# Zero halves of five query and key buffers: written by transfers in ScalarE's queue instead of by the engines

## The chip, the cores and the metric

The kernel runs on one core of a Trainium2 chip. The metric is the device time of one execution in microseconds (us). Executions are timed from outside, and one further execution is recorded by the hardware profiler, which gives the trace that is read here.

## The reference

Two layers in float32, one after the other:

```python
# attention: q, k, v of (B 4, H 8, S 768, D 64); 8 global keys, a window of 96
scores = (q @ k.T) / sqrt(D) - slope[h] * dist      # dist is capped at n_local for global keys
scores = where(is_global | is_local, scores, -1e9)
a = exp(scores - max); a = a / (sum(a) + 1e-9)
x = (a @ v)  # heads side by side: (B, S, 512)
# channel mix: x_prev is x moved by one position
xk = mu_k * x + (1 - mu_k) * x_prev;  xr = mu_r * x + (1 - mu_r) * x_prev
out = sigmoid(xr @ w_r) * (relu(xk @ w_k) ** 2 @ w_v)
```

The weights are float64 values, which the kernel gets as pairs of 32-bit words and turns into float32 itself.

## The kernel before

The sequence is cut into 24 tiles of 128 queries (B times NT = 6). One loop of steps goes over the tiles. In a step the tile's scores are made for two heads at a time (`scores`, matmuls of L421 and L422 into the PSUM tile `s`), VectorE adds the bias pattern and takes the maximum (L430), ScalarE takes the exponential (L431), TensorE turns the result (`transposes`, L461), ScalarE copies it out (L465), and `weighted` multiplies it by v (L486). The channel mix of a pair of tiles (`ffn`, lines L529 to L531) is fed in between. Ten blocks of weight words are loaded in the first steps (L181, L182; 1 MB each), put together on VectorE (L210 to L212), and split into a high and a low part (L216 on ScalarE, L230 to L234 on TensorE, ScalarE and VectorE).

The first six tiles are "native": their scores are float32 matmuls over 128 partitions, of which the 64 even ones hold q or k (`qr[0:128:2]`, loaded by L338 and L339 from SyncE's queue) and the 64 odd ones must be zero. Their buffers are used in turn: two query buffers `q_zero[0]`, `q_zero[1]` (in the trace `qz`) and three key buffers `k_ring[0]` to `k_ring[2]` (`kz`). They are zeroed once, ahead of the first loads, by `zero_fill`: the table `PLAN["Z"]` names an engine for each, D for VectorE (L311), A for ScalarE (L309, two instructions a buffer), and GpSimd where the table says nothing (L306). A whole buffer is zeroed, so that the load of its even partitions must come behind.

At the start VectorE also makes the distances for the bias patterns: GpSimd writes counters (`iota`, L136 to L138), L139 turns them into floats in `btmp`, L78 takes in the two sizes (`sizes_w`, loaded by the first transfer in SyncE's queue, L71), and the chain ends in L149 and L164. From these, ScalarE, VectorE and GpSimd make `pat0` (L153, L155) and `pat` (L170, L172); ScalarE also makes `minus` (L85), which only the weights need. `mus` (L89) is the first transfer in ScalarE's queue. Ten matmuls on `zeros` (L116) run on TensorE while it has nothing else to do.

The order within each engine is not the order of the code: a scheduler sets it by a model of the times, but for SyncE's queue, which is kept in program order for the first six steps. Each engine then works through its list in order. Transfers share eight completion semaphores, DMAHW0 to DMAHW7, which are given out in turn; a transfer waits before it is issued for the last user of its semaphore to land.

Of the kernel before, what the change touches and what calls it, by code (L numbers as in the profile page):

```python
# [9 lines left out]
F32 = mybir.dt.float32  # L10
# [9 lines left out]
B, H, S, D = 4, 8, 768, 64  # L20
# [8 lines left out]
W = GMAX + BACK + 128  # L29
# [7 lines left out]
PLAN = {  # L37
    "HI": 'AAAAAAAAAA',
    "LOW": 'PPDPDDDDDD',
    "RC": 'AAAAAAAAAAAAAAAAAAAA',  # L40
    "ER": set(),
    "ET": (),
    "XC": (),
    "Z": {('q', 0): 'D', ('q', 1): 'A', ('k', 1): 'A'},
    "P0": 'DADDADAD',
    "GD": 0,
    "GO": (1, 1),
# [15 lines left out]
def tile_biased_attention_channel_mix(ctx: ExitStack, tc: tile.TileContext, qT, kT, v, n_sizes, mu_kr, w_k, w_v, w_r, q_rows, k_rows, v_rows, slopes, out):  # L63
    nc = tc.nc
    vec, act, pool, pe = nc.vector, nc.scalar, nc.gpsimd, nc.tensor
# [16 lines left out]
    ident = const.tile([128, 128], F32, name="ident")  # L82
    make_identity(nc, ident)
    minus = const.tile([128, 128], F32R, name="minus")
    nc.scalar.mul(minus, ident, -1.0)  # L85

    mus = const.tile([128, 2, 4], F32, name="mus")
    mus1 = const.tile([128, 2, 4], F32, name="mus1")
# [8 lines left out]
    kw_pool = fast.enter_context(tc.tile_pool(name="kw", bufs=2))  # L97
    q_pool = fast.enter_context(tc.tile_pool(name="qp", bufs=2))
# [13 lines left out]
    zeros = const.tile([128, 256], BF16, name="zeros")  # L112
# [3 lines left out]
        pe.matmul(idle, zeros[:, 0:128], zeros.unsqueeze(1).broadcast_to([128, 2, 256]), start=True, stop=True)  # L116

    pat = const.tile([128, H, W], BF16, name="pat")
# [177 lines left out]

    state = {}  # L300


    def zero_fill(which, i, whole):
        e = PLAN["Z"].get((which, i), "P")
        if e == "P":
            pool.memset(whole, 0.0)  # L306
        elif e == "A":
            for h in (0, 4):
                act.copy(whole[:, h : h + 4, :], zeros[:, 0:128].unsqueeze(1).broadcast_to([128, 4, 128]))  # L309
        else:  # L310
            vec.memset(whole, 0.0)  # L311

    q_zero, k_ring = [], []
    for i in range(3):
        if i < 2:
            q_zero.append(q_pool.tile([128, H, 128], F32, name=f"qz_{i}", tag="qh"))
            kz = kw_pool.tile([128, H, W], F32, name=f"kz_{i}", tag="kw").rearrange("p h w -> p (h w)")[:, 0 : H * 128]
            kz = kz.rearrange("p (h w) -> p h w", h=H)
            zero_fill("q", i, q_zero[i])
        else:  # L320
            kz = q_pool.tile([128, H, 128], F32, name=f"kz_{i}", tag="ql")
        zero_fill("k", i, kz)
        k_ring.append(kz)
    k_first = const.tile([128, H, GMAX], F32, name="k_first")

    def first_keys(n):
# [516 lines left out]
```

## Time and profile before

| | us |
|---|---|
| median of 3 runs | 499.98 (498.32 to 500.26) |
| the profiled execution | 496.85 |
| its span, from the first to the last instruction | 495.1 |
| TensorE busy in the span | 485.0 (98%) |
| VectorE busy | 348.9 (70%) |
| ScalarE busy | 335.8 (68%) |

1.75 us of the profiled execution lie outside the span. TensorE is busy nearly throughout, but busy shares are means over stages with different limits, so the first stage has to be read by itself.

### The profile page before, as it was taken

Reading aid. Unit: us, or ns where it says so; the run is one execution under the profiler, and the core shown is the slowest. Engines: PE = TensorE matmul, PEld = TensorE weight load, DVE = VectorE, ACT = ScalarE, POOL = GpSimd, SP = SyncE. Lnnn points to the kernel's source line nnn. Section 1 sums busy time; section 2 is a strip of 40 time slices with the busy share of each in tenths; the row PEclk is TensorE's granted clock in tenths of the full one; section 3 lists DMA queues with packets and bytes.
Section 4 is the critical chain, followed back from the end, with each engine's and each line's share of the span. In section 5 each row is a group of like instructions: output and inputs, shape, how many; then the busy total and the mean of one; then the engine's idle time right before and its main releaser. Section 6 shows DMA issues by size and latency. Waiting matters only on the chain.

```text
span 495.1 us, 10282 instructions
## 1 busy us (share of the span) xinstructions
PE 485.0 (98%) x3614; PEld 432.1 (87%) x3614; DVE 348.9 (70%) x839; ACT 335.8 (68%) x852; POOL 204.2 (41%) x331
## 2 busy tenths in 40 slices
PE   7999999999999999999999999999999999999995
PEld 5688988998988988988988998998998998988984
DVE  7999988857577777667677677777677656446431
ACT  8999866557397478468488578477487477595450
POOL 4202043638375454554564554644655633203000
PEclk9999999999999999999999999999999999999998
DMA  6997343811525216216306306406405125574401
GB/s 249 377 312 305 71 93 82 208 45 38 135 73 136 65 47 169 77 36 153 103 24 158 94 4 167 122 2 161 129 2 139 49 72 165 185 263 164 144 25 51
DMA packets 22587, 60.59 MB, mean 122 GB/s; under 512 B 3296, under 2 KB 4576, under 8 KB 22016
## 3 DMA queue, kind: packets, MB, share of 16 engines
q1 hardware_dynamic: 22384, 59.85, 41.1%
q8 instruction: 31, 0.51, 0.4%
q14 instruction: 28, 0.23, 0.1%
q10 hardware_dynamic: 144, 0.00, 0.0%
HBM read 53.55 MB, written 6.29 MB: 121 GB/s over the span
## 4 chain that ended last, share of the span: by engine, by line
PE 95%; DVE 2%; ACT 1%; issue 0%; ACTq 0%
PE kp L529 9%; PE kp L530 9%; PE kp L531 9%; PE vps L529 9%; PE vps L531 9%; PE vps L530 9%; PE av L486 8%; PE t L461 8%; PE z L529 5%; PE z L530 4%; PE z L531 4%; PE s L425 3%; PE s L424 3%; PE s L422 2%; PE s L421 2%; PE rest L230 1%
## 5 line engine op out<-in xcount | busy, mean ns | idle before, releaser
L449 POOL TENSOR_SCALAR e<-e,r 128x232 f32<-128x232 f32 (+1 forms) x144 | 68.7, 495 | 122.8 <-DVE r L443 86.8
L431 ACT ACTIVATE e<-e,nmax 128x232 f32<-128x232 f32 (+1 forms) x192 | 89.6, 469 | 36.7 <-DVE nmax L430 36.1
L529 PE MATMUL kp<-xk_hi,wk 128*128 128x256 f32 x384 | 107.9, 282 | 0.0
L530 PE MATMUL kp<-xk_lo,wk 128*128 128x256 f32 x384 | 107.3, 280 | 0.0
L531 PE MATMUL kp<-xk_hi,wk 128*128 128x256 f32 x384 | 107.2, 280 | 0.0
L430 DVE CUSTOM_DVE_ANT_0 e<-s,pat 128x232 f32<-128x232 f32 (+1 forms) x192 | 64.2, 374 | 27.9 <-PE s L425 25.8
L529 PE MATMUL vps<-wv,kk_hi 128*128 128x512 f32 (+1 forms) x200 | 76.8, 385 | 0.0
L531 PE MATMUL vps<-wv,kk_lo 128*128 128x512 f32 (+1 forms) x200 | 76.7, 383 | 0.0
L530 PE MATMUL vps<-wv,kk_hi 128*128 128x512 f32 (+1 forms) x200 | 76.4, 382 | 0.0
L530 PEld LDWEIGHTS kp<-xk_lo,wk 128*128 128x128 f32 x384 | 72.1, 188 | 0.8 <-DVE xk_lo L522 0.2
L529 PEld LDWEIGHTS kp<-xk_hi,wk 128*128 128x128 f32 x384 | 72.0, 188 | 0.7 <-ACT xk_hi L521 0.3
L531 PEld LDWEIGHTS kp<-xk_hi,wk 128*128 128x128 f32 x384 | 72.1, 188 | 0.0
L465 ACT COPY et<-t 128x256 f32<-128x256 f32 (+1 forms) x176 | 53.3, 354 | 23.4 <-PE t L461 23.2
L461 PE MATMUL t<-ident,e 128*128 128x128 f32 x352 | 54.5, 275 | 0.4 <-ACT et L465 0.3
L557 DVE TENSOR_TENSOR kk<-kp,kk 128x512 f32<-128x512 f32 x48 | 32.9, 688 | 29.8 <-ACT kk L556 29.4
L559 DVE TENSOR_TENSOR kk_lo<-kk,kk_hi 128x512 fp32r<-128x512 f32 x48 | 36.7, 769 | 24.1 <-ACT kk_hi L558 23.2
L461 PEld LDWEIGHTS t<-ident,e 128*128 128x128 f32 x352 | 40.3, 135 | 6.2 <-ACT et L465 0.6
L558 ACT CAST kk_hi<-kk 128x512 fp32r<-128x512 f32 x48 | 29.7, 622 | 22.2 <-DVE kk L557 21.9
L531 PEld LDWEIGHTS vps<-wv,kk_lo 128*128 128x128 f32 x200 | 37.6, 188 | 7.5
L529 PEld LDWEIGHTS vps<-wv,kk_hi 128*128 128x128 f32 x200 | 37.6, 189 | 6.7 <-issue 0.2
L530 PEld LDWEIGHTS vps<-wv,kk_hi 128*128 128x128 f32 x200 | 37.7, 189 | 6.5
L424 PE MATMUL s<-kw,qh 128*128 128x232 f32 (+1 forms) x144 | 40.4, 306 | 0.0
(119 smaller groups left out, 1068.2 us busy)
## 6 DMA issues: line engine op xcount, KB each, us to landing
qraw<-in_qT_dram SPq DMA_DIRECT2D x36, 256.0 KB
kraw<-in_kT_dram SPq DMA_DIRECT2D x36, 256.0 KB
out_dram<-sig SPq DMA_DIRECT2D x23, 256.0 KB
va<-in_v_dram SPq DMA_DIRECT2D x20, 240.0 KB
vb<-in_v_dram SPq DMA_DIRECT2D x20, 208.0 KB
w<-in_w_k_dram SPq DMA_DIRECT2D x4, 1024.0 KB
w<-in_w_v_dram SPq DMA_DIRECT2D x4, 1024.0 KB
again<-in_w_k_dram SPq DMA_DIRECT2D x8, 512.0 KB
```

Source lines behind the costliest of these rows:

```text
L424: pe.matmul(o, s["qh"][:, h, :], s["kw"][:, h, c0:W], start=True, stop=False)
L430: biased[n, hp] = vec.tensor_tensor_reduce(out=e[:, :w], in0=o, in1=p[:, h, :], op0=ALU.add, op1=ALU.min, scale=-0.125, scalar=3.0e38, acc ...
L431: act.activation(e[:, :w], e[:, :w], AF.Exp, bias=s["nmax"][:, h : h + 1], scale=-1.0, accum_out=s["sum"][:, h : h + 1])
L449: pool.tensor_scalar(e[:, :w], e[:, :w], r[:, u : u + 1], 1.0, op0=ALU.mult, op1=ALU.mult)
L461: s["turned"] = pe.transpose(pt[0:p, c : c + 128], e[:, k * 128 : k * 128 + p], ident)
L465: act.copy(dst, pt[0:p, k * 256 : k * 256 + 256].rearrange("p (u q) -> p u q", u=2)[:, :, q:128])
L486: pe.matmul(o, vt[:, h * 64 : (h + 1) * 64], et[0:p, c : c + 128 - q], start=k == 0, stop=k == nb - 1)
L529: pe.matmul(o, sh, mh, start=first, stop=False)
L530: pe.matmul(o, sh, ml, start=False, stop=False)
L531: pe.matmul(o, sl, mh, start=False, stop=last)
L557: vec.tensor_mul(kk, pv, kk)
L559: rest = vec.tensor_sub(kkl[:, 2 * fp : 2 * fp + 2, :], kk, kkh[:, 2 * fp : 2 * fp + 2, :])
```

## The change

The zeros of all five buffers come from transfers. Each is issued from ScalarE's queue and copies 512 bytes of zeros, eight times for each partition, from 64 partitions of the tile `zeros` into the 64 odd partitions of a buffer: 64 x 8 pieces of 512 bytes, 256 KB a buffer. The even partitions are no longer written beforehand. The code of `zero_fill` stands further ahead, and `minus` is put behind the last of the five transfers.

```diff
-    "Z": {('q', 0): 'D', ('q', 1): 'A', ('k', 1): 'A'},
+    "Z": {('q', 0): 'S', ('k', 0): 'S', ('q', 1): 'S', ('k', 1): 'S', ('k', 2): 'S'},
...
     minus = const.tile([128, 128], F32R, name="minus")
-    nc.scalar.mul(minus, ident, -1.0)
...
+    filled = []
+
+    def zero_fill(which, i, whole):
+        e = PLAN["Z"].get((which, i), "P")
+        if e == "P":
+            pool.memset(whole, 0.0)
+        elif e == "S":
+            filled.append(nc.scalar.dma_start(whole[1:128:2], zeros.bitcast(F32)[0:64].unsqueeze(1).broadcast_to([64, H, 128])))
...
+    with tc.issue_after(filled[-1].ins):
+        act.mul(minus, ident, -1.0)
```

The first rows of ScalarE's list before (each row a line of the code, an operation, and what it writes and reads; semaphores that it waits for in brackets):

```order
L89 DMA mus<-in_mu_kr_dram 128x8
L309 ACT_TABLE_LOAD
L309 CAST qz_182<-zeros 128x512 [waits DVE_49]
L309 CAST kz_183<-zeros 128x512 x2
L85 ACTIVATE minus<-ident 128x128 [waits Pool_49]
L153 ACTIVATE pat_137<-btmp 128x128 [waits DVE_49]
L170 ACTIVATE pat<-btmp 128x232 [waits DVE_49]
```

And with the change, where line numbers differ (L127 is the new transfer, L181 the old L153, L198 the old L170; qz_135 and qz_139 are the two query buffers, kz_136, kz_140 and kz_143 the three key buffers):

```order
L88 DMA mus<-in_mu_kr_dram 128x8
L127 DMA qz_135<-zeros 64x8x128 [waits DVE_49]
L127 DMA kz_136<-zeros 64x8x128
L127 DMA qz_139<-zeros 64x8x128
L127 DMA kz_140<-zeros 64x8x128 [waits DMAHW1_49]
L127 DMA kz_143<-zeros 64x8x128 [waits DMAHW3_49]
L146 ACT_TABLE_LOAD
L146 ACTIVATE minus<-ident 128x128 [waits Pool_49]
L181 ACTIVATE pat_147<-btmp 128x128 [waits DVE_49]
L198 ACTIVATE pat<-btmp 128x232 [waits DVE_49]
```

Ahead of the table load stand five transfers in place of one, and two of them wait for the landing of an earlier transfer; the table load and the patterns moved behind these waits.

SyncE's list before, from its second transfer on:

```order
L338 DMA qz_178<-in_qT_dram 64x1024 [waits DVE_49]
L339 DMA kz_179<-in_kT_dram 64x1024 [waits Pool_49]
L338 DMA qz_182<-in_qT_dram 64x1024 [waits Activation_49]
L339 DMA kz_183<-in_kT_dram 64x1024 [waits Activation_49]
L374 DMA va_199<-in_v_dram 128x512
L181 DMA w_0_211<-in_w_k_dram 128x2048
L181 DMA w_1_213<-in_w_k_dram 128x2048 [waits DMAHW0_49]
L338 DMA qz_178<-in_qT_dram 64x1024 [waits DMAHW2_49,DMAHW1_49,PE_49]
L339 DMA kz_188<-in_kT_dram 64x1024 [waits Pool_49]
```

And with the change (L344 is the old L338, L345 the old L339, L209 the old L181):

```order
L344 DMA qz_135<-in_qT_dram 64x1024
L345 DMA kz_136<-in_kT_dram 64x1024
L344 DMA qz_139<-in_qT_dram 64x1024
L345 DMA kz_140<-in_kT_dram 64x1024 [waits DMAHW0_49]
L380 DMA va_197<-in_v_dram 128x512 [waits DMAHW2_49]
L209 DMA w_0_209<-in_w_k_dram 128x2048 [waits DMAHW4_49]
L209 DMA w_1_211<-in_w_k_dram 128x2048 [waits DMAHW5_49]
L344 DMA qz_135<-in_qT_dram 64x1024 [waits DMAHW6_49,PE_49]
L345 DMA kz_143<-in_kT_dram 64x1024 [waits DMAHW7_49]
```

The order is the same. The waits for the zeroing engines are gone, and the transfers from the fourth on now wait for the landing of earlier transfers.

TensorE's list at the first scores, before:

```order
L422 MATMUL s_0_202<-kz_179,qz_178 128x128 [waits DMAHW2_49,DMAHW3_49,DVE_49,Pool_49]
L422 MATMUL s_3_255<-kz_179,qz_178 128x128 [waits DVE_49]
L461 MATMUL t_0_274<-ident,e_0_205 128x128 [waits Activation_49]
L461 MATMUL t_1_306<-ident,e_2_224 128x128 [waits Activation_49]
L421 MATMUL s_0_279<-kz_179,qz_182 128x104 [waits DMAHW4_49,DVE_49,Pool_49]
L422 MATMUL s_0_279<-kz_183,qz_182 128x128 [waits DMAHW5_49]
```

And with the change (L428 is the old L422, L427 the old L421, L467 the old L461):

```order
L428 MATMUL s_0_200<-kz_136,qz_135 128x128 [waits DMAHW4_49,DMAHW5_49,DMAHW3_49,DMAHW2_49]
L428 MATMUL s_3_253<-kz_136,qz_135 128x128 [waits DVE_49]
L427 MATMUL s_0_277<-kz_136,qz_139 128x104 [waits DMAHW6_49,DMAHW7_49,DVE_49,Pool_49]
L428 MATMUL s_0_277<-kz_140,qz_139 128x128 [waits DMAHW1_49,DMAHW0_49]
L467 MATMUL t_0_272<-ident,e_0_203 128x128 [waits Activation_49]
```

The first scores of a tile wait for four transfers in place of two and two engines. Two matmuls of the second tile's scores moved ahead of the first transposes. Further differences in the order, by a few places, go on in the lists of TensorE, VectorE and ScalarE through the first six tiles; later the lists are the same.

## Rows read from the trace of the kernel before

**Rows 1.** The page: busy time of each engine, and the packets of all transfers.

```profile
PE 485.0 (98%) x3614; PEld 432.1 (87%) x3614; DVE 348.9 (70%) x839; ACT 335.8 (68%) x852; POOL 204.2 (41%) x331
DMA packets 22587, 60.59 MB, mean 122 GB/s; under 512 B 3296, under 2 KB 4576, under 8 KB 22016
```

**Rows 2.** Stages: us, busy us of each engine, PE clock, DMA share, GB/s.

```profile
0.00:3.00 3.00, 1.94 (x5) 0.74 (x6) 2.00 (x3) 1.82 (x3) 2.42 (x12) 1.00 0.04 2
3.00:5.00 2.00, 1.89 (x6) 0.55 (x4) 1.96 (x9) 1.85 (x5) 0.91 (x3) 1.00 0.74 211
5.00:8.00 3.00, 1.49 (x11) 1.33 (x12) 3.00 (x20) 1.99 (x8) 1.55 (x5) 1.00 0.80 277
8.00:12.00 4.00, 3.94 (x35) 3.66 (x34) 2.21 (x16) 4.00 (x21) 0.47 (x2) 1.00 1.04 414
12.00:15.00 3.00, 2.68 (x24) 2.30 (x22) 3.00 (x15) 3.00 (x14) 1.72 (x2) 1.00 1.00 401
15.00:50.00 35.00, 33.81 (x290) 26.89 (x288) 34.58 (x89) 32.21 (x96) 4.64 (x6) 1.00 0.91 322
50.00:72.00 22.00, 22.00 (x168) 20.76 (x167) 21.94 (x43) 16.61 (x45) 6.17 (x6) 1.00 0.42 92
72.00:495.00 423.00, 417.25 (x3090) 375.84 (x3088) 280.24 (x653) 274.28 (x667) 186.32 (x299) 1.00 0.37 102
```

**Rows 3.** The chain that ended last, first 9.5 us: start, us, what.

```profile
1.17 0.91 DVE qz L311
2.08 1.78 DVE btmp L139
3.86 0.07 DVE words L78
5.72 0.27 DVE btmp L149
6.01 0.71 ACT pat L153 x3
7.87 1.17 ACT e L431 x6
```

**Rows 4.** Timeline, first 7.2 us: start, us, engine, line, operation [idle before].

```profile
0.75 0.39 SPq L71 DMA_DIRECT2D sizes_w<-in_n_sizes_dram  x1
1.17 1.28 ACT L309 ACT_TABLE_LOAD   x1 [1.17 <-PEq L833]
1.78 1.84 POOL L306 MEMSET kz<- 128x1024 f32 x2
2.11 0.57 SPq L338 DMA_DIRECT2D qz<-in_qT_dram  x1
2.47 1.14 ACT L309 CAST qz<-zeros 128x512 f32<-128x512 bf16 x2
2.76 0.55 SPq L339 DMA_DIRECT2D kz<-in_kT_dram  x1
4.55 0.30 ACT L85 ACTIVATE minus<-ident 128x128 fp32r<-128x128 f32 x1
6.03 1.13 PE L422 MATMUL s<-kz,qz 128*128 128x128 f32 x8 [1.14 <-DVE btmp L149]
```

**Rows 5.** Timeline of TensorE and VectorE, 9 to 50 us.

```profile
9.25 0.47 PE L421 MATMUL s<-kz,qz 128*128 128x104 f32 x2
12.32 0.68 DVE L210 TENSOR_SCALAR wa<-w 128x1024 int32<-128x1024 int32 x1
15.15 1.04 PE L421 MATMUL s<-kz,qz 128*128 128x104 f32 x4
49.71 0.44 PE L421 MATMUL s<-kz,qz 128*128 128x104 f32 x2 [0.97 <-issue]
```

**Rows 6.** A load in pieces of 512 bytes: its issue (timeline), and its window.

```profile
58.02 1.25 SPq L353 DMA_DIRECT2D kraw<-in_kT_dram  x2
60.00:62.50 2.50, 2.50 (x25) 2.50 (x24) 2.50 (x4) 1.81 (x3) 0.88 (x1) 1.00 1.12 203
```

More of the change, by code (lines that the diff above doesn't have):

```diff
@@ L116, in tile_biased_attention_channel_mix @@
         pe.matmul(idle, zeros[:, 0:128], zeros.unsqueeze(1).broadcast_to([128, 2, 256]), start=True, stop=True)
+    filled = []
[5 more added lines that the diff above has]
+            filled.append(nc.scalar.dma_start(whole[1:128:2], zeros.bitcast(F32)[0:64].unsqueeze(1).broadcast_to([64, H, 128])))
+        elif e == "A":
+            for h in (0, 4):
+                act.copy(whole[:, h : h + 4, :], zeros[:, 0:128].unsqueeze(1).broadcast_to([128, 4, 128]))
+        else:
+            vec.memset(whole, 0.0)
+    q_zero, k_ring = [], []
+    for i in range(3):
+        if i < 2:
+            q_zero.append(q_pool.tile([128, H, 128], F32, name=f"qz_{i}", tag="qh"))
+            kz = kw_pool.tile([128, H, W], F32, name=f"kz_{i}", tag="kw").rearrange("p h w -> p (h w)")[:, 0 : H * 128]
+            kz = kz.rearrange("p (h w) -> p h w", h=H)
+            zero_fill("q", i, q_zero[i])
+        else:
+            kz = q_pool.tile([128, H, 128], F32, name=f"kz_{i}", tag="ql")
+        zero_fill("k", i, kz)
+        k_ring.append(kz)
+    with tc.issue_after(filled[-1].ins):
+        act.mul(minus, ident, -1.0)
     pat = const.tile([128, H, W], BF16, name="pat")
@@ L300, in tile_biased_attention_channel_mix @@
     state = {}
[L303 to L323, printed above, removed]
     k_first = const.tile([128, H, GMAX], F32, name="k_first")
```

## The prediction

> **What bounds the kernel now.** I read the page first: TensorE is busy 485.0 of 495.1 us [rows 1], so only time that TensorE loses can be won. Where it loses any is seen in the stages [rows 2]. From 72 us on it is busy 417.25 of 423 us, and the lists of the changed kernel are the same there: nothing can change but the moment at which that stage begins. Ahead of it the reader should look at VectorE: 3.00 of 3 us busy from 12 to 15, 34.58 of 35 from 15 to 50, 21.94 of 22 from 50 to 72. TensorE is nearly as full there (33.81 of 35), and where it stops, as for 0.97 us before 49.71 [rows 5], the profile names no other engine's idle time behind it while VectorE is still full. So I take it that from 12 us on VectorE, which runs without a gap in a fixed order, sets the pace, and that whatever makes the work at 12 us late or early moves the rest by as much. The change acts ahead of that, so I read the chain that ended last [rows 3] and the timeline of the start [rows 4], and then the transfers: 414 and 401 GB/s at a share of 1.0 from 8 to 15 us [rows 2], so the loads run at the engines' limit just when the first weights and tiles come in.
>
> The chain begins on VectorE with the zeros of `qz` (0.91 us), goes on with the cast L139 (1.78 us of the chain) and short steps to L149, which ends at 5.99. Then it moves to ScalarE: patterns from 6.01, exponentials from 7.87 [rows 3]. Sums are made against the profiled execution, 496.85 us; the median of the runs is 499.98, 3.13 us above it, and I add the sum to the median.
>
> **What is removed.** VectorE loses 0.91 us [rows 3]. The cast lay beside GpSimd's two zeroings, 1.78 to 3.62 [rows 4], and ended just after them; without them I give it what steps of similar kind take in the chain, 0.27 us for 128 columns at L149 [rows 3], so 0.3 to 0.8 us for 352 columns. Taken alone that moves the chain up by about 1.8 us (from 3.86 to some 2.1). But L78 comes next in the list and needs the transfer of the sizes. In the first 3 us 2 GB/s are moved [rows 2], 6 KB, which is the sizes and `mus` together; so the sizes land between about 3.0 and the 3.86 at which L78 runs now. The steps from L78 to the end of L149 take 5.99 - 3.86 = 2.1 us, so L149 ends between 5.1 and 6.0. I take 5.6: 0.4 us early. ScalarE loses four casts, two times 1.14 us [rows 4]; it had waited for L149 from 4.85 to 6.01, so that time was covered and is worth nothing by itself. GpSimd's 1.84 us are worth nothing beyond the cast, since its patterns wait for L164. The loads of q and k no longer wait for zeroing: the first can be issued at 1.14, when the sizes' issue ends, instead of 2.11.
>
> **What is added, first on ScalarE.** Five issues of about 0.6 us each (the load in pieces of 512 bytes took 1.25 us for two [rows 6]). Three can go out from 1.15 to 3.0; the fourth waits for the sizes to land; the fifth shares a semaphore with an early transfer and waits for that one. From the order in which the eight are given out (`mus`, sizes, q0, zeros of q0, k0, zeros of k0, and so on in turn) I read it as the zeros of the first query buffer. Behind it stand the table load (1.28 us), `minus` (0.30 us) [rows 4] and all of ScalarE's patterns. When do the first zeros land? The first key load was issued at 2.76 and the scores that need it began at 6.03 [rows 4], 3.3 us later, while q0 was in flight ahead of it. By that row the zeros, issued at 1.15, land at 4.4. If they move at the 203 GB/s of the 512-byte load [rows 6] and share the engines with q0 (the loads moved 211 GB/s at this point [rows 2]), 1.0 us more: 5.4. Then 0.6 + 1.28 + 0.30 = 2.2 us until the first pattern: 6.6 to 7.6 against 6.01 now. I take 7.3, nearer the upper end because the row for such pieces is the slow one. **ScalarE's chain: +1.3 us**, and the 0.4 us that VectorE wins is lost in waiting for it. Queued behind the waiting transfer on ScalarE are the patterns of three heads that VectorE's first steps need, and all exponentials; for these wait the transposes, and so TensorE.
>
> **Then on the transfers.** Five times 256 KB are 1.31 MB more. At 203 GB/s [rows 6] that is 6.5 us of all engines; at the 414 GB/s of the large loads [rows 2], 3.2 us. The scores of tile 1 began at 9.25 [rows 5] and now need four zeroings and four loads. The four loads are 1.05 MB, 4.2 us at some 250 GB/s (211 and 277 in the stages in which they run [rows 2]). The four zeroings take 5.2 us at 203 GB/s, and the first bytes come at about 2.4, 1.3 us after the first issue (the same distance as from 2.11 to the beginning of traffic at a little over 3). If all of it goes one after another, it ends at 11.8; with some overlap, for the share of the engines was 0.74 to 0.80 there [rows 2], at about 11, plus half a microsecond to be seen: 11.5 against 9.25. **Tile 1: +2.3 us**, in which the +1.3 us of ScalarE's chain is contained.
>
> The first weights are behind all this. Summing the stages [rows 2], 0.43 MB have been moved by 5 us and 1.26 MB by 8; the first 2.36 MB, up to the first block, were in by 8 + 1.10 / 0.414 = 10.7 us, and VectorE took them up at 12.32 [rows 5]. With 6.5 us of zeroing, less the 1.0 us by which transfers begin earlier and about 1.1 us in which the engines stood idle from 3 to 8, the block is in 4.4 us later, at 15.1, and usable at about 15.6. VectorE would ask for it at 12.32 + 2.3 = 14.6: **+1.0 us**. The loads of tile 2 are next, in front of the scores at 15.15 [rows 5]; 3.93 MB were in at about 14.6, and 4.4 us later is 19.0, about as late as the scores then ask (15.15 + 3.3, and half a microsecond to be seen): another few tenths, which I leave out against what the reordered scores of TensorE may fill. Later weights have 2 us of slack and more by the same sum. I take 0.7 for the weights, because some of the zeros will be moved beside loads. Sum: 2.3 + 0.7 = +3.0 us, and 499.98 + 3.0 = **503.0 us**. If the fourth and fifth zeroings are faster than I think, the sum is +1.5; with the wait for tile 2 in full, +4.5.
>
> **Rivals.** A change of less than 0.5%, 2.5 us, can't be told from none here.
>
> First, the cover holds. If the zeros move at 400 GB/s and in the gaps of the loads, the first land at 4.4, ScalarE's patterns begin at 6.6 less what the faster issue saves, and tile 1's eight transfers end at 2.4 + 2.6 + 2.6 = 7.6, ahead of 9.25; the first weights come 3.2 - 2.1 = 1.1 us later, at 11.8 and seen at 12.3, just when wanted. What stays is +0.4 us, from -0.5 to +1.5: 500.4. For it: the share of the engines was 0.74 to 0.80 from 3 to 8 us. Against it: the only load in such pieces in this trace ran at half rate. The Trainium skill ("DMA: Bandwidth & Descriptors", section "Why small descriptors are slow (HBM only)") says that copies within the on-chip memory don't pay for small pieces; by that rule this rival is the likely one. No row here shows such a copy.
>
> Second, the zeros starve. If the engines take turns between the two queues piece by piece, a 512-byte piece for each 4 KB piece of a load, the zeros of q0 are through only when 32 load pieces per engine have passed, which is q0, k0, q1, k1, v0 (24 pieces of 1.31 MB, some 4.5 us) and part of the first weights: landing at about 9, those of k0 at 11 and later. First scores at 11 instead of 6.03, ScalarE's patterns at 11.2 instead of 6.01: +5 us, and up to +10 if the zeros of tile 1 wait for the second weights too. 505 to 510. The same page's section "Queues, rings and completion order" says that an engine goes round the queues packet by packet; the trace of before has only one busy queue and can't show it. For it speaks that the page of the profile counts 512-byte pieces as packets like others: 4576 - 3296 = 1280 packets from 512 bytes to 2 KB [rows 1].
>
> Third, the other side: the head start passes through. If the sizes land at 3.0 and the wait of the fifth transfer is over by 3.5, patterns begin at about 5.1 and tile 0's scores at 5, and all of the 0.91 us and part of the cast are won: -0.9 to -1.8 us, and with TensorE's new order up to -3. It decides at the landing of the first zeros, which would have to take 2.3 us from their issue where the first key load took 3.3. 498.2.
>
> That the zeroing isn't moved at all can't be: the list of ScalarE shows it.
>
> **Chances.** The forecast 0.42 (of it 0.13 under +2.5 us), cover holds 0.30, starving 0.20, head start 0.08 (0.05 of it beyond -2.5 us). Slower by over 0.5%: 0.29 + 0.20 = 0.49. Within: 0.13 + 0.30 + 0.03 = 0.46. Faster: 0.05. The range leaves out half of the head start and of the lowest covered cases below, and the worse half of starving above: 499.0 to 507.0. The forecast's own range is 501.5 to 504.5.
>
> **What would show it.** ScalarE's fifth transfer issued later than 4.4, table load behind it, first pattern (the old L153) after 6.6; L149's end before 5.99 and VectorE then idle; the cast under 0.8 us. Tile 1's first scores after 10.5 and the first L210 idle for a transfer. VectorE full from there to some 75 us, and the stage after it as long as now. I am wrong if the fifth transfer goes out by 4.0, if tile 1's scores begin by 9.3, or if the lateness of the start is gone by 50 us because TensorE's list has slack that I don't see.

## The result and the profile after

The changed kernel takes 503.62 us (median of 5 runs, 502.96 to 504.62), the kernel before 499.36 beside it (497.49 to 500.26): a ratio of 1.0089, 95% interval 1.006 to 1.0117; the medians are 4.3 us apart, and the interval times 499.36 is 3.0 to 5.8 us. The forecast was 503.0. The profiled execution is one of the longer ones, 504.56 us.

The page of the changed kernel first: busy time of the engines, packets, and ScalarE's queue of transfers, with its share of all 16 engines' span.

```profile
span 502.7 us, 10283 instructions
PE 489.1 (97%) x3614; PEld 435.5 (87%) x3614; DVE 347.0 (69%) x838; ACT 333.3 (66%) x848; POOL 200.6 (40%) x329
DMA packets 25227, 61.90 MB, mean 123 GB/s; under 512 B 3376, under 2 KB 7216, under 8 KB 24656
q10 hardware_dynamic: 2784, 1.32, 1.0%
```

Against [rows 1] VectorE has 1.9 us less to do and ScalarE 2.5, and the span is 7.6 us longer. The zeros are 2640 of the packets and took 1.0% of 502.7 us, 5.0 us of all engines for 1.31 MB: some 260 GB/s, between the 203 and the 414 of the forecast.

The stages, with the columns of [rows 2] (us; busy us of TensorE, its weight loads, VectorE, ScalarE, GpSimd; granted clock; share of the transfer engines; GB/s):

```profile
3.00:5.00 2.00, 1.90 (x6) 0.55 (x4) 0.84 (x6) 0.00 (x0) 0.20 (x1) 1.00 0.90 272
5.00:8.00 3.00, 0.00 (x0) 0.00 (x0) 2.47 (x13) 0.23 (x1) 1.34 (x4) 0.93 1.01 294
8.00:12.00 4.00, 2.90 (x13) 2.89 (x14) 1.02 (x8) 3.99 (x14) 0.44 (x2) 0.50 1.16 307
12.00:15.00 3.00, 2.54 (x12) 2.25 (x12) 1.02 (x8) 2.34 (x12) 0.24 (x1) 0.50 0.97 372
15.00:50.00 35.00, 34.20 (x277) 28.03 (x276) 32.69 (x94) 30.29 (x93) 4.44 (x6) 0.96 0.97 339
50.00:72.00 22.00, 20.75 (x184) 18.92 (x180) 22.00 (x47) 19.75 (x55) 4.21 (x3) 1.00 0.50 130
```

ScalarE is idle from 3 to 5 us and nearly so from 5 to 8, where it had worked 1.85 and 1.99 us [rows 2]. VectorE, full from 12 us on before, has 1.02 of 3 us to do there. TensorE does nothing from 5 to 8 us, and from 8 to 15 its granted clock is 0.50, the 1.2 GHz level, where it was 1.00.

The timeline of the start (columns as in [rows 4]). L127 are the transfers of zeros, L167 the old L139, L177 the old L149, L181 the old L153, L428 and L427 the old L422 and L421, L238 the old L210:

```profile
1.20 0.69 ACTq L127 DMA_DIRECT2D qz<-zeros  x1
1.59 0.41 DVE L167 CAST btmp<-btmp 128x352 f32<-128x352 int32 x1 [0.59 <-POOL btmp L166]
4.12 1.40 ACTq L127 DMA_DIRECT2D kz<-zeros  x1
4.12 0.17 DVE L78 CAST words<-sizes_w 128x4 f32<-128x4 int32 x1 [2.12 <-DMA sizes_w<-in_n_sizes_dram]
5.76 1.97 ACTq L127 DMA_DIRECT2D kz<-zeros  x1
5.93 0.35 DVE L177 SCALAR_TENSOR_TENSOR btmp<-btmp,sizes 128x128 f32<-128x128 f32 x1
7.76 1.28 ACT L146 ACT_TABLE_LOAD   x1 [7.76 <-DVE pat L183]
9.10 3.88 PE L428 MATMUL s<-kz,qz 128*128 128x128 f32 x16 [4.20 <-DMA kz<-zeros]
9.28 0.69 ACT L181 ACTIVATE pat<-btmp 128x128 bf16<-128x128 f32 x3
11.02 0.39 ACT L437 ACTIVATE e<-e,nmax 128x128 f32<-128x128 f32 x1
13.13 0.24 POOL L325 TENSOR_SCALAR kz<-k_first 128x64 f32<-128x64 f32 x1 [3.78 <-PE s L428]
13.43 0.76 PE L427 MATMUL s<-kz,qz 128*128 128x104 f32 x2 [0.46 <-POOL kz L325]
18.84 0.69 DVE L238 TENSOR_SCALAR wa<-w 128x1024 int32<-128x1024 int32 x1
```

Three transfers go out from 1.2 to 3.9 us; their issues take 0.69, 0.80 and 1.12 us. The fourth waits for the sizes, which land at 4.10, and its issue takes 1.40. The fifth waits for the zeros of the first query buffer, which land at 5.74 by the trace's completion records; its issue begins at 5.76, takes 1.97 and is out at 7.74. So the two waits for a landing cost ScalarE's list only 0.25 and 0.24 us; what holds it is that the issues themselves grow, from 0.69 to 1.97 us. The table load stands behind them, and the first pattern starts at 9.28 in place of 6.01 [rows 3]. (The profile puts the table load down to VectorE; the issues are what stands in front.) TensorE's first scores wait for the zeros of k0 to 9.10, against 6.03 [rows 4], and take 3.88 us for 16 matmuls. Tile 1's scores then wait for GpSimd's copy into `kz` (L325), and that for the last of these 16. The chain that ended last shows the way through the zeros of k0 in three pieces:

```profile
1.20 0.69 ACTq L127
1.93 7.04 DMA kz<-zeros
9.10 3.89 PE s L428 x16
```

The lateness then stays. VectorE's idle time up to the last scores of the native tiles, first before and then after (same columns as the stages):

```profile
0.00:62.90 62.90, 58.66 (x471) 48.15 (x472) 59.65 (x170) 56.43 (x170) 12.81 (x28) 1.00 0.77 262
```

```profile
0.00:70.20 70.20, 62.45 (x471) 51.57 (x472) 58.82 (x171) 55.39 (x167) 10.67 (x27) 0.93 0.80 258
```

VectorE does 0.8 us less and idles 11.4 us in place of 3.3: 7.3 us in sum, and by 7.3 us the last scores are later. From these scores (62.5 and 69.8) to the end of the span it is 432.6 and 432.9 us: the later stage is untouched. That is one execution of each; the medians are 4.3 us apart.

### The profile page after: what moved, and what is told of

It is laid out like the page before. It is cut to its first block, busy times and chain, and to the rows that moved or that the text cites. A ratio compares the mean times of both kernels' runs of the same rounds, so it can differ in the third digit from the quotient of the medians.

```text
span 502.7 us, 10283 instructions
## 1 busy us (share of the span) xinstructions
PE 489.1 (97%) x3614; PEld 435.5 (87%) x3614; DVE 347.0 (69%) x838; ACT 333.3 (66%) x848; POOL 200.6 (40%) x329
## 4 chain that ended last, share of the span: by engine, by line
PE 89%; DVE 7%; DMA 1%; ACT 1%; issue 1%; ACTq 0%; POOL 0%; POOLq 0%
PE kp L535 9%; PE kp L537 9%; PE kp L536 9%; PE vps L535 9%; PE vps L537 9%; PE vps L536 9%; PE av L492 7%; PE t L467 7%; PE z L535 5%; PE z L537 4%; PE z L536 4%; PE s L431 3%; PE s L430 3%; DVE wa L239 2%; DVE e L436 2%; DMA kz<-zeros 1%
## 5 line engine op out<-in xcount | busy, mean ns | idle before, releaser
L455 POOL TENSOR_SCALAR e<-e,r 128x232 f32<-128x232 f32 (+1 forms) x144 | 65.7, 474 | 127.0 <-DVE r L449 93.7
L467 PE MATMUL t<-ident,e 128*128 128x128 f32 x352 | 55.8, 277 | 1.0 <-ACT e L437 0.6
L565 DVE TENSOR_TENSOR kk_lo<-kk,kk_hi 128x512 fp32r<-128x512 f32 x48 | 37.8, 788 | 23.8 <-ACT kk_hi L564 22.9
L467 PEld LDWEIGHTS t<-ident,e 128*128 128x128 f32 x352 | 40.7, 136 | 8.3 <-ACT e L437 1.6
```

Source lines behind the costliest of these rows:

```text
L455: pool.tensor_scalar(e[:, :w], e[:, :w], r[:, u : u + 1], 1.0, op0=ALU.mult, op1=ALU.mult)
L467: s["turned"] = pe.transpose(pt[0:p, c : c + 128], e[:, k * 128 : k * 128 + p], ident)
L565: rest = vec.tensor_sub(kkl[:, 2 * fp : 2 * fp + 2, :], kk, kkh[:, 2 * fp : 2 * fp + 2, :])
```

## The experiments

Each kernel was timed against the kernel before on the same chip.

| kernel | median us | ratio to before | 95% interval |
|---|---|---|---|
| the change (5 transfers, 10 idle matmuls) | 503.62 | 1.0089 | 1.0060 to 1.0117 |
| 5 transfers, 22 idle | 502.50 | 1.0072 | 1.0043 to 1.0101 |
| 5 transfers, 18 idle | 502.59 | 1.0086 | 1.0055 to 1.0117 |
| 4 transfers, 10 idle | 501.62 | 1.0040 | 1.0016 to 1.0064 |
| 4 transfers, 18 idle | 499.41 | 0.9985 | 0.9964 to 1.0006 |
| pieces of 4 KB | 503.47 | 1.0080 | 1.0050 to 1.0111 |
| 5 transfers in SyncE's queue | 501.89 | 1.0064 | 1.0040 to 1.0088 |
| engines zero, code moved | 500.40 | 1.0028 | 1.0004 to 1.0052 |
| transfers for q1, k1, k2 only | 500.80 | 1.0035 | 1.0012 to 1.0058 |
| transfers for q0, k0 only | 502.98 | 1.0077 | 1.0046 to 1.0108 |
| q0, k0 only, 14 idle | 501.38 | 1.0045 | 1.0018 to 1.0071 |
| q1, k1, k2 in SyncE's queue | 508.74 | 1.0196 | 1.0151 to 1.0240 |
| before, 12 idle | 499.32 | 0.9985 | 0.9961 to 1.0009 |

**The fifth transfer and the clock: four corners.** The first corner is the change itself. The second has no fifth transfer:

```diff
-    "Z": {('q', 0): 'S', ('k', 0): 'S', ('q', 1): 'S', ('k', 1): 'S', ('k', 2): 'S'},
+    "Z": {('q', 0): 'S', ('k', 0): 'S', ('q', 1): 'S', ('k', 1): 'S'},
```

> The changed kernel without its fifth transfer: the zeros of k2 are written by GpSimd, so that four transfers stand in ScalarE's list ahead of its table load and its patterns, and none has to wait for an earlier one to land. Theory 'the wait of the fifth transfer holds ScalarE's list': the table load comes at 4.5 to 5.5 us in place of 7.8, the patterns start at 6 to 7 us in place of 9.3; the first scores still start at 7.5 to 9 us, when the zeros of k0 land, and the time is 502 to 503 us. Theory 'the fourth holds it as much, or the landing of the zeros alone sets the time': patterns come sooner or not, the first scores start at 8 to 9 us at half clock as in the changed kernel, and the time stays at 503 to 504 us.

```profile
5.40 1.28 ACT L146 ACT_TABLE_LOAD   x1 [5.40 <-DVE btmp L175]
6.93 0.71 ACT L181 ACTIVATE pat<-btmp 128x128 bf16<-128x128 f32 x3
8.60 2.30 PE L428 MATMUL s<-kz,qz 128*128 128x128 f32 x11 [3.09 <-DMA kz<-zeros]
```

In its timeline the table load comes 2.4 us sooner and the patterns 2.4 sooner, though the first scores still wait for k0's zeros to 8.60. The time is 501.62: 2.4 us of the 4.3 are gone by the ratios, though the intervals still touch (1.0016 to 1.0064, 1.0060 to 1.0117). The first theory's landmarks hold; its time, 502 to 503, was a little high. What is gone with the fifth transfer is its issue of 1.97 us and a wait of 0.24. (The fourth still waits, for the sizes, to 4.03.)

The third corner changes nothing but the idle matmuls at the start (the order of all other instructions stays):

```diff
-    for i in range(10):
+    for i in range(22):
```

> The changed kernel with 22 instead of 10 idle matmuls at the start, nothing else: TensorE is then kept busy up to the time at which its first scores can start (9.1 us in the changed kernel), where it had been idle from 4.9 to 9.1 us and was granted half clock (0.50) from 8 to 17.5 us. Theory 'the clock carries a large part of the loss': the granted clock stays at 1.00 from 8 to 18 us, the first sixteen score records take about 1.95 us in place of 3.88, tile 1's scores start at 11.5 to 12 us in place of 13.4, tile 2's about 3 us sooner than 21.8, and the time falls from 503.6 to about 500.5 to 501.5 us. Theory 'the late patterns and late exponentials set it': the scores are quicker but tile 1 waits all the same, since ScalarE and VectorE still come to the first exponentials at 11 us, and the time stays at 503 to 504 us.

502.50, between the two. Eight scores took 1.13 us and tile 1 began at 12.43, but TensorE was then idle from 19 to 21 us, and the clock fell there instead:

```profile
20.00:21.00 1.00, 0.00 (x0) 0.00 (x0) 1.00 (x2) 1.00 (x7) 0.00 (x0) 0.96 1.13 262
21.00:22.00 1.00, 0.96 (x5) 0.97 (x5) 0.78 (x4) 1.00 (x6) 0.00 (x0) 0.50 1.06 268
```

So this run settles little. The corner with four transfers was therefore run with 18 (`range(18)`), and then, as its counterpart, the one with five:

> The kernel with four transfers of zeros (k2 by GpSimd) and 18 instead of 10 idle matmuls, the order of the other instructions unchanged against it. Theory 'the wait of the fifth transfer and the clock are two separate parts of the loss': this one loses neither, the first sixteen scores take about 2.3 us in place of 3.8, and the time is 0.8 to 1.5 us below that of the four transfers with ten idle matmuls (501.6), some 500 to 501 us. Theory 'the clock is not worth a measurable part': within 0.6 us of 501.6.

> The changed kernel (five transfers) with 18 instead of 10 idle matmuls, the order of the other instructions unchanged against it: the fourth corner beside the changed kernel, the one with four transfers, and the one with four transfers and 18 idle matmuls. Theory 'the wait of the fifth transfer costs by itself, whatever the clock': the table load still comes at 7.5 us or later, the patterns at 9 us, and the time is 2 to 4 us above the kernel before, some 501.5 to 503 us, that is 2 us or more above the corner with four transfers. Theory 'with the clock up the fifth transfer costs nothing': 499.5 to 500.5 us.

With four transfers the idle matmuls give 2.7 us, all that was left of the loss (0.9985) and more than was expected. With five they give nothing measurable (1.0086 against 1.0089), so the two parts don't simply add up. The timelines, first four and then five transfers, both with 18:

```profile
5.37 1.28 ACT L146 ACT_TABLE_LOAD   x1 [5.37 <-DVE btmp L175]
8.54 1.13 PE L428 MATMUL s<-kz,qz 128*128 128x128 f32 x8 [1.32 <-DMA kz<-zeros]
9.60 0.40 ACT L437 ACTIVATE e<-e,nmax 128x128 f32<-128x128 f32 x1 [0.76 <-DVE nmax L436]
```

```profile
7.54 1.28 ACT L146 ACT_TABLE_LOAD   x1 [7.54 <-DVE pat L183]
8.94 1.13 PE L428 MATMUL s<-kz,qz 128*128 128x128 f32 x8 [1.54 <-DMA kz<-zeros]
10.79 0.39 ACT L437 ACTIVATE e<-e,nmax 128x128 f32<-128x128 f32 x1
```

The scores are 0.4 us apart, at full clock in both; the exponentials are 1.2 us apart, and with five transfers ScalarE's list is what is late: they come without a wait for VectorE. The pair costs 1.01% (5.0 us) in the medians; in the two profiled executions, 497.8 and 499.8 us of span, only 2.0 of it is seen. Without the fifth transfer GpSimd has a buffer to zero, and the lists of TensorE, VectorE and ScalarE differ in many rows; how much of the 5.0 us that carries was not separated from the fifth issue.

**Small pieces.** The zeros come from a tile with 4 KB of zeros in each partition:

```diff
-            ...zeros.bitcast(F32)[0:64].unsqueeze(1).broadcast_to([64, H, 128])))
+            ...wide_zeros))
```

> The changed kernel with the zeros copied from a tile of zeros that is 4 KB long in each partition instead of one that is read again and again in pieces of 512 bytes: the same bytes, an eighth of the packets or less, the order of the engines' lists unchanged apart from one memset of 64 partitions x 1024 numbers on VectorE ahead of it (about 1 us). Theory 'it is the small pieces that make the zeros land late': ScalarE's queue takes 2 to 3 us of sixteen engines in place of 5.0, the zeros of k0 land by 6 to 7 us in place of 9.0, the patterns start at 7 to 8 us and the time falls to about 501 us. Theory 'it is the bytes and the sharing with the loads': the packets are fewer but the zeros land at 8.5 us or later, and the time stays within 1 us of 503.6.

An eighth of the pieces, 0.8% of the span (4.0 us) in place of 1.0%, and the first scores 0.9 us sooner, when k0's zeros are in:

```profile
q10 hardware_dynamic: 544, 1.32, 0.8%
8.22 1.20 PE L430 MATMUL s<-kz,qz 128*128 128x128 f32 x4 [2.71 <-DMA kz<-wide_zeros]
```

The time is the same, as the second theory said, though the zeros land a little before its 8.5 us. The pieces do count for the landing: VectorE's additional memset puts the transfer of k0's zeros 0.7 us later (issued at 2.65 in place of 1.93), and from issue to landing it takes 5.4 us in place of 7.0. ScalarE's issues are shorter too (0.52 to 1.12 us in place of 0.69 to 1.97), but its fifth waits from 5.28 to 6.15 for the first zeros, so that the table load comes at 7.26, only 0.5 us sooner. The Trainium skill ("DMA: Bandwidth & Descriptors", section "Why small descriptors are slow (HBM only)") says that copies within the on-chip memory don't suffer from small pieces; by these two rows 512 bytes cost about a quarter more engine time than 4 KB, so in engine time the measurement says otherwise; in the kernel's time they cost nothing that shows. What it was to bring, a cover that holds, did not follow from it.

**Another queue.** All five transfers in SyncE's queue, each ahead of the load of its buffer (`minus` then no longer stands behind a transfer):

```diff
-            filled.append(nc.scalar.dma_start(whole[1:128:2], ...))
+            filled.append((which, i, whole))
...
+                for which, i, whole in filled:
+                    if (which, i) == (name, n):
+                        nc.sync.dma_start(whole[1:128:2], ...)
```

> The changed kernel with the same five transfers of zeros put into SyncE's queue, each just ahead of the load of the same tile's data, in place of ScalarE's queue. ScalarE's list is then free of transfers and of the wait for them. Theory 'ScalarE's list is what made tile 1 late': patterns start near 6 us as before the change, and the time comes back to 499.5 to 501 us. Theory 'the zeros are late because their bytes lie in the way of the loads, whoever issues them': the first scores still start at 7.5 to 9 us, TensorE is idle for 3 us or more ahead of them, its clock falls to 0.50 again, and the time is 502 to 505 us; loads of q1, k1, va and the weights come 2 us or more later.

The time is 501.89. The table load is back at 1.17 and the patterns start at 5.74, sooner than before the change, but the first scores wait to 7.88, now for the load, and a block of weights is late as well:

```profile
7.88 0.55 PE L432 MATMUL s<-kz,qz 128*128 128x128 f32 x1 [2.37 <-DMA kz<-in_kT_dram]
28.99 0.69 DVE L237 TENSOR_SCALAR wa<-w 128x1024 int32<-128x1024 int32 x1 [2.15 <-DMA w<-in_w_k_dram]
```

So a free ScalarE list alone doesn't bring the time back: in one queue the zeros push everything behind them. Neither theory's number is met in full, and the interval overlaps that of the change.

**Which zeros.** A control with no transfer of zeros: the table of before (`{('q', 0): 'D', ('q', 1): 'A', ('k', 1): 'A'}`), the code where the change puts it:

> The zeros written by the engines as before the change (q0 by VectorE, q1 and k1 by ScalarE, k0 and k2 by GpSimd), but with the code in the place that the change gives it, ahead of the patterns: no transfer of zeros, and the lists of the engines in the new order where the place alone moves them. Theory 'the transfers cost the time': 499 to 500.5 us, first scores at 6 to 6.5 us and the clock at 1.00. Theory 'the new order of the lists costs it': 502 us or more.

The time is 500.40, a ratio of 1.0028: the place of the code alone goes with 1.4 us (0.2 to 2.6), through the order that it brings or through TensorE, whose first scores are slow in this profiled execution (454 ns each from 6 to 7 us, 284 in the kernel before). VectorE's cast now stands behind the wait for the sizes. The changed kernel has its cast ahead of it, so the control doesn't stand for its order, only for what an order can cost.

Then the transfers of the later buffers alone (`"Z": {('q', 0): 'D', ('q', 1): 'S', ('k', 1): 'S', ('k', 2): 'S'}`) and of the first tile alone (`{('q', 0): 'S', ('k', 0): 'S', ('q', 1): 'A', ('k', 1): 'A'}`):

> The changed kernel with the zeros of the first tile (q0, k0) written by VectorE and GpSimd again, and the three later ones (q1, k1, k2) by transfers in ScalarE's queue. Nothing that the first scores need is then a transfer of zeros, and three transfers stay in flight beside the loads with none that waits for an earlier one. Theory 'the first tile waiting for its own zeros is the loss': first scores start at 6 to 7 us at full clock, patterns at 6 to 7 us, and the time is 499 to 501 us. Theory 'the bytes in the way of the loads are the loss': q1, k1, va and the weights land late, tile 1's scores still start at 11 us or later, and the time is 502 us or more.

> The changed kernel with only the first tile's zeros (q0, k0) as transfers, and q1, k1 by ScalarE and k2 by GpSimd as before the change. Two transfers stand at the head of ScalarE's list and none waits; 0.5 MB in place of 1.3 MB shares the engines with the loads. Theory 'the first tile waiting for its own zeros is the loss': the zeros of k0 land at 6 to 8 us, the first scores are 1 to 2 us late against 6.0, and the time is 500.5 to 502 us, above that of the kernel with the three later ones alone. Theory 'the bytes are the loss': with two fifths of the bytes two fifths of the loss, some 501 us, and below that of the kernel with the three later ones.

The times are 500.80 and 502.98: three transfers cost nothing measurable beyond the control, two cost 2.4 us more by the ratios (the intervals, 1.0004 to 1.0052 and 1.0046 to 1.0108, just touch). Yet the later buffers' zeros are in the way too: in that kernel the first scores wait for the load of k0, issued at 2.72 as in the control, where they ran at 6.04:

```profile
8.48 3.02 PE L428 MATMUL s<-kz,qz 128*128 128x128 f32 x12 [3.13 <-DMA kz<-in_kT_dram]
```

So first scores that are 2.4 us late need not be a loss: the theory of the first tile's wait met its time here (499 to 501), but not its landmarks. And the kernel with the first tile's zeros has them at 7.44 and its patterns at 7.03, sooner than the four transfers, and takes longer; the theory that gave it the loss for its wait was right in the order of the two kernels, but its time (500.5 to 502) was 1 us too low, and the wait is not the whole cause. Its matmuls from 8 to 11 us, and their stage (whose granted clock of 1.00 is explained in the last section); then the matmuls of its twin with 14 idle ones (`range(14)`), whose other instructions stand in the same order:

```profile
L428 PE MATMUL s<-kz,qz 128*128 128x128 f32 x15 | 3.5, 429 | 0.0
8.00:11.00 3.00, 3.00 (x15) 2.96 (x14) 1.60 (x12) 2.68 (x13) 1.08 (x4) 1.00 0.92 340
```

```profile
L428 PE MATMUL s<-kz,qz 128*128 128x128 f32 x17 | 2.5, 282 | 0.2 <-DVE nmax L436 0.2
```

> The kernel with the zeros of the first tile alone as transfers, and 14 instead of 10 idle matmuls, the order of the other instructions unchanged against it. With ten, its profiled execution ran all scores to 17 us at 421 ns a matmul, the length they have at half clock, and it took 503.0 us although its first scores and patterns came sooner than in the kernel with four transfers (501.6). Theory 'the slow matmuls are why it is no better': matmuls of 275 ns from 7.5 us on and 500.5 to 501.5 us. Theory 'something else in its list': 502.5 to 503.5 us.

The time is 501.38: the matmuls have full speed, and two thirds of the loss over the control are gone (0.0032 of 0.0049). The intervals of the two overlap (1.0046 to 1.0108, 1.0018 to 1.0071), so that the slow matmuls are the cause is likely and not shown.

**The later buffers in SyncE's queue**, q0 and k0 by the engines:

> The kernel with the first tile's zeros written by VectorE and GpSimd and the three later ones (q1, k1, k2) by transfers in SyncE's queue, each just ahead of its own load. ScalarE's list holds no transfer and no zeros at all. Theory 'the first tile waiting for its own zeros is the loss': first scores at 6 to 6.5 us, the clock at 1.00, and the time within 0.7 us of the kernel before (499 to 500); if ScalarE's freed time is worth something, 498 to 499. Theory 'the bytes in the way of the loads': tile 1's scores late by 1 us or more and 500.5 to 502 us.

The time is 508.74, which no theory gave. The first scores start at 5.93 and the patterns at 6.44, about as before. The loss comes later: VectorE sits idle for 1.88 us before 12.35, for 3.28 before 25.48, when the scores of tile 2 are late, and for 3.07 before 79.08, and TensorE's clock is at 0.50 for 3.4 us from 8.4 and again from 18.7. All lists differ from those of the kernel with the same three transfers in ScalarE's queue, so order and queue are not told apart here, and the cause stays open.

**The kernel before with two more idle matmuls** (`range(12)`):

> The kernel before the change with 12 instead of 10 idle matmuls, all else as it was apart from some twenty rows on TensorE, VectorE and ScalarE that change places. Theory 'the executions of the kernel before differ because TensorE's clock rises sooner in some than in others, and two more idle matmuls make it rise in more of them': 0.5 to 1 us below the kernel before and a narrower spread. Theory 'the rise is a matter of the execution alone': within 0.5 us of it and the same spread.

The time is 499.32, a ratio of 0.9985: no measurable gain, and about the same spread (497.09 to 500.83). The second theory holds. No version here beats the kernel before by more than its interval.

## Why the prediction was right

**Right in place and direction, and in part lucky in the number.** VectorE carried the lateness of the first 18 us through to 70, and the stage behind it is as long as before. The cast took 0.41 us (0.3 to 0.8 forecast); in the control, where it runs after GpSimd's zeroing and not beside it, 0.34. The fifth transfer went out long after 4.4 us with the table load behind it, patterns after 6.6, tile 1 after 10.5. That the fifth transfer costs is shown by taking it away, with the limit that the order changes too. But 503.0 is a sum of 2.3 for tile 1 and 0.7 for the weights, and the one was too small, by another path, and the other nil; that the sum lies 0.6 us from the median (3.0 forecast, the medians 4.3 apart) is luck.

**ScalarE's chain, +1.3 us, was too small: it is +3.3** (9.28 against 6.01). The semaphore was read rightly, and the landing that it waits for was nearly right: 5.74 against 4.4 to 5.4. What was mis-sized is the issue behind it, put at 0.6 us from [rows 6] and 1.97 in the run. ScalarE's issues grew one after another while four transfers of zeros and three loads were in flight, and SyncE's did too: the second query load, which waits for nothing, took 1.30 us, against 0.47 before the change. Why an issue takes longer then is not shown.

**L149, 0.4 us early, was 0.3 late** (it starts at 5.93, against 5.63 before). The bound "between 3.0 and the 3.86" for the sizes held for an empty path. They landed at 4.1 beside the other transfers; in the control without transfers L78 starts at 3.56.

**Tile 1, +2.3 us, was +4.2** (13.43 against 9.25), and by another path. The forecast was the landing of tile 1's own eight transfers, at 11.5; the last of them landed at 12.17. What tile 1 waited for was tile 0: its first scores began 3.1 us late, when k0's zeros were in, a landing that the sum has no term for, and the 16 took 3.88 us where before the change they took 2.8, a pause of 0.5 included. At full speed eight take 1.13 [rows 4], so 1.6 us of the 3.88 are the clock, for which the forecast had no term either. The half microsecond from a landing until it is seen is in no run: k0's zeros landed at 8.96 and the scores began at 9.10.

**The first weights, +0.7 us, were nil:** the block landed at 16.07 (15.1 forecast), but tile 1 is so late that L238 waits for no transfer at 18.84.

**The rivals.** "The cover holds" is out by the time and by k0's zeros. "The zeros starve" gave 11 for the first scores and 11.2 for the patterns, from landings at about 9 and 11; they came at 9.10 and 9.28, from landings at 5.74 and 8.96. Its turns of one piece each are not what the trace shows. From 5 to 8 us, with both queues busy, ScalarE's queue (q10) and SyncE's (q1) moved about the same number of bytes in very different numbers of packets (packets, MB, share of 16 engines):

```profile
q10 hardware_dynamic: 841, 0.42, 55.3%
q1 hardware_dynamic: 144, 0.46, 46.0%
```

"The head start" shows in VectorE alone: the sizes and the fifth transfer consumed it.

## What to carry to other kernels

A transfer that is issued from the queue of a computing engine costs that engine its list for as long as the issue takes, and with many transfers in flight that was 2 us and not 0.6; so count the transfers ahead of the first compute instruction, and read each issue's length apart from the wait in front of it. Work moved off an idle engine onto shared transfer engines at the start of a kernel can delay every load beside it, even loads whose own path was not touched. When a start is changed, look at what TensorE does in the gap, and compare the mean length of its matmuls, not the mean clock alone, before a microsecond is put down to the change.

## What the runs showed of the hardware that was not expected

**After the same ten idle matmuls TensorE is fast in one execution and slow in another.** They took 634 ns each at first and 380 later. In the profiled execution of the changed kernel that happened at about 4.2 us, in that of the first tile's transfers not while they ran:

```profile
L115 PE MATMUL idle<-zeros 128*128 128x512 bf16 x2 | 0.6, 380 | 0.0
```

```profile
L115 PE MATMUL idle<-zeros 128*128 128x512 bf16 x3 | 1.5, 634 | 0.0
```

(Both from 4.5 to 5 us.) The granted clock reads 1.00 in both, and also where scores took 429 ns above, near the 449 ns of the changed kernel from 8 to 11 us at a granted 0.50. That 1.00 is no measurement: the trace holds changes of the clock alone, and what lies ahead of the first one counts as 1.00. The first entry, to full clock, stands at 4.16 us in the changed kernel's trace and at 16.75 in that of the first tile's transfers, in both just where the matmuls get short (in [rows 2], too, the 1.00 of the first 4.1 us is of this kind). So at the start a mean matmul duration tells the clock, and the mean clock of an execution leaves out what it lost before its first entry.

**Where the record shows a fall, the time of the kernel before goes with it.** Of its 88 executions that were timed beside the experiments, 45 had a mean granted clock of 0.996 or more and a median of 498.27 us; 30 had 0.993 to 0.995 and 500.07; 13 had 0.992 or less and 501.71. It is not so in every kernel: with four transfers and ten idle matmuls the five executions at 0.996 or more have a median of 502.02, the seven others 501.23. A high mean can also belong to an execution whose clock rose late, as the trace of the first tile's transfers shows (0.996, 503.50 us). All 12 of the four transfers with 18 idle matmuls had 0.997 or more, and lie within 1.5 us (498.40 to 499.92). Of the executions at 0.996 or more, those with 18 idle matmuls have a median of 499.41 with four transfers and 502.24 with five (5 of 6): 2.8 us apart, with the change of order in it.

**What a long fall costs is not shown.** In the changed kernel the clock fell to 1.2 GHz at about 7.6 us, after TensorE had been idle from 4.9, and rose at 17.8. Its two executions with a mean clock of 0.986 took 504.6 us, the two with 0.993 took 503.0 and 503.1, and the one with 1.000 took 503.6. With 18 idle matmuls, at full clock through the first scores of the profiled execution, the ratio stayed the same. So ten microseconds at half speed cost little here; that TensorE had waits to fill is a likely reason.
